# Two of the seven W2 operands of an attention + MLP kernel: read from stored bf16 copies, or cast from W2 by every pair

## The chip, the cores and the metric

The kernel runs on one core of a Trainium2 chip. The metric is the device time of one execution in microseconds (us), lower is better. Engines are named as the profile names them: PE (TensorE), PEld (its weight loads), DVE (VectorE), ACT (ScalarE), POOL (GpSimd), SP (SyncE, which here only issues DMAs).

## The reference

Eight batches of grouped-query attention (16 query heads, 4 key/value heads, 384 tokens, head size 64), whose output is the input of one MLP block:

```python
x   = softmax(q @ k^T / 8) @ v                     # per batch, then [384 tokens, 1024]
a1  = alpha1 * x + beta1
tok = einsum('ts,bsd->btd', w_tok, a1)
u   = x + lam * tok
a2  = alpha2 * u + beta2
ch  = relu(a2 @ w_ch1) @ w_ch2                     # w_ch1 [1024, 4096], w_ch2 [4096, 1024]
out = u + lam * ch
```

Inputs and output are float32. W1 and W2 below are `w_ch1` and `w_ch2`.

## The kernel before

**Pairs.** The batches are worked two at a time: four pairs (`ps`, and `i` in `pair`, 0 to 3). The two big matrix products of a pair are each done with seven half-size products in place of eight (Strassen's scheme with sums shared): the two batches are the halves on one side, and the four quarters of a weight matrix are those on the other. So each pair has a *first product* (activations by W1, relu) and a *second product* (by W2), each of seven parts numbered 1 to 7.

**First product of pairs 1 to 3** (`pair`, the loop over `g`, L818 to L864). Eight groups g = 0 to 7, each of 14 steps of four matmuls (`SEQ1`, L831). A group needs two W1 chunks of 512 KB (bf16 in SBUF), which POOL's DMAs read from the float32 W1 and cast on the way (`load_w1`, L183). They go into a ring `w1` of six slots; the loads for group g+3 are issued when group g gives its two slots back (`free`, `pump`). DVE makes the sums of W1 chunks for group g+1 while PE works on group g (`sum_w1`, L510 and L515, at steps k = 2, 5, 8 and 11). The two adds at L838 read the PSUM tiles `Y`, into which part 4, the last two steps of the group, accumulates further.

**Second product** (L876 to L941). Seven parts in the order of `PLACE2`: 1, 2, 6, 5, 3, 7, 4. Each needs an operand made of W2 (2 MB in bf16, four tiles of 512 KB): parts 1, 2 and 3 use the plain quarters "11", "21" and "22" of W2, the other four use differences of quarters. Pair 0 builds all of them: it loads the quarters with a cast (`load_w2`), DVE forms the differences (`sum_w2`), and SP writes every operand as bf16 into 28 tiles `w2s` in HBM (`keep_w2`, L494; quarter "21" goes there by a casting DMA, `cast_w2`). Pairs 1 to 3 read the tiles back in order n = 0 to 27 with SP's DMAs (`fetch`, L528), n // 4 being the place of the part in the order above: n = 0 to 3 are part 1, n = 16 to 19 part 3. They go into the six `w1` slots, which the first product gives back from group 5 on, and into three slots of `pad`.

**Where the order comes from.** The instruction order on every engine is the order of the program text (`tc.manual_schedule`). `queue` holds the W1 and W2 loads in one list; `pump` issues from its head whenever a slot is given back, at that point of the program. So a `fetch` stands in SP's stream (SP's queue) at the place where its slot was given back, and SP stops there until the slot is free; a `load_w1` stands likewise in POOL's. The rest comes from `plan`, a table of (pair, product, step): among others `load_next` (POOL's DMAs for k, q and v of the next two batches), and `put_flips`, which in the first product of pairs 0 to 2 puts on SP the transposing DMAs for the next batch's attention: `flip_k` (L170, all of kT, 12 blocks of 128 x 128) and four `flip_q` (L174, a quarter of qT each, 6 blocks). A `flip_q` can start when its quarter of `q_raw` has been loaded by POOL (L436). After the first product the attention of the next two batches is woven into the second product, batch 2 ps + 2 first. Pair 3 has no next pair, so it has no flips and no attention.

**DMA queues.** POOL's DMAs, casting ones and the accumulating stores to `out` (L442), are q0 (software_dynamic) in the profile; SP's plain loads, stores and transposes are q1 (hardware_dynamic). A DMA of SP or POOL also waits until the eighth DMA before it on the same engine has landed.

```python
queue += [(load_w1, c) for c in order1[4:]] + [(fetch, i, n) for n in range(SLOTS - 2)] + heads[:2]
...
put_flips(ps, 0, c, (44, 46, 50, 54, 58) if ps == 0 else range(76, 86, 2))
```

The five flips of pairs 1 and 2 thus stand at steps 76 to 84 of the first product's 112, in groups 5 and 6; group 5 gives its two slots back at steps 80 and 81.

Of the kernel before, what the change touches and what calls it, by code (L numbers as in the profile page):

```python
# [13 lines left out]
def kernel(  # L14
# [21 lines left out]
    nc = tc.nc  # L36
# [81 lines left out]
    SLOTS = 7 * NH // 4  # L118
    w2s = [tc.dram_tile([P, NDT * CW * P], bf, name=f"w2s{i}") for i in range(SLOTS)]
    PLACE2 = {o: i for i, o in enumerate((1, 2, 6, 5, 3, 7, 4))}  # L120

    def by_tok(ap):
        return ap.rearrange("(p st) d -> p st d", st=NST)
# [342 lines left out]
    raw = {}  # L466
# [4 lines left out]
    def w2_block(name, c):  # L471
        kh, dw = int(name[0]) - 1, int(name[1]) - 1
        return w2src[:, kh * NH + 4 * c:kh * NH + 4 * c + 4, dw * 512:(dw + 1) * 512]

    def stored(c):
        return w2s[4 * PLACE2[2] + c]

# [13 lines left out]
            nc.gpsimd.dma_start(out=at.rearrange("p (a c) -> p a c", a=4), in_=w2_block(name, c))  # L491

    def keep_w2(o, c):
        nc.sync.dma_start(out=w2s[4 * PLACE2[o] + c], in_=raw[{1: "11", 3: "22", 5: "12", 6: "12", 7: "11", 4: "again"}[o], c][1])  # L494

    def sum_w2(o, c):
        at = lambda name: raw[name, c][1]
        to, x, y = {5: ("12", "12", "11"), 6: ("12", "22", "12"), 7: ("11", "12", "11"), 4: ("again", "again", "12")}[o]
        tt(out=at(to), in0=at(x), in1=at(y), op=SUB)
        keep_w2(o, c)  # L500
# [17 lines left out]
    w2_slots, w2_at = {}, {}  # L518
# [3 lines left out]
    def place(slot):  # L522
        return ring[:, slot] if slot < RING else pad[:, (slot - RING) * 2048:(slot - RING + 1) * 2048]

    def fetch(i, n):
        w2_slots[i, n] = slot = (pad_free if n in PADDED else w1_free).pop(0)
        w2_at[i, n] = place(slot)
        nc.sync.dma_start(out=w2_at[i, n], in_=w2s[n])  # L528

    def free(slot):  # L530
        (w1_free if slot < RING else pad_free).append(slot)
# [46 lines left out]
    for i in range(1, NB):  # L578
        heads = [(load_w1, c) for c in order1[:4]] if i + 1 < NB else []
        queue += [(load_w1, c) for c in order1[4:]] + [(fetch, i, n) for n in range(SLOTS - 2)] + heads[:2]  # L580
        queue += [(fetch, i, n) for n in (SLOTS - 2, SLOTS - 1)] + heads[2:]
# [190 lines left out]
    def pair(i):  # L772
# [102 lines left out]
        where = {2: (0, 0), 3: (0, 1), 7: (1, 1), 4: (1, 0)}  # L875
        for k, o in enumerate(PLACE2):  # L876
            whole = not last and o != 4
# [69 lines left out]
    with tc.manual_schedule(engines=order):  # L947
# [123 lines left out]
        def put(ps, phase, at, *m):  # L1071
            plan.setdefault((ps, phase, at), []).append(m)
# [25 lines left out]
        for c in range(4):  # L1098
            put(0, 0, (50, 72, 74, 44)[c], load_w2, "11", c)
            put(0, 0, (6, 14, 42, 46)[c], cast_w2, "21", c)  # L1100
            put(0, 1, (41, 43, 45, 47)[c], keep_w2, 1, c)
            put(0, 1, 38 + 2 * c, keep_w2, 3, c)
            put(0, 1, (9, 10, 13, 15)[c], sum_w2, 5, c)
            put(0, 1, (20, 21, 25, 26)[c], sums_first_hid, 2, c)
            put(0, 1, (28, 30, 31, 34)[c], sums_first_hid, 4, c)
            put(0, 1, (37, 40, 41, 43)[c], sum_w2, 6, c)
            put(0, 1, (44, 45, 49, 50)[c], sums_first_hid, 3, c)
            put(0, 1, (51, 54, 57, 58)[c], sum_w2, 7, c)
            put(0, 1, (61, 64, 68, 71)[c], last_w2, c)
        for u, o in ((77, 5), (79, 7), (81, 6)):  # L1110
            put(0, 1, u, sum_w1, 0, o)
        for ps in range(NB - 1):
            c = 2 * ps + 2
# [100 lines left out]
```

## Time and profile before

| | |
|---|---|
| median of 3 runs | 732.88 us (731.51 to 733.32) |
| the profiled execution's own time | 731.92 us |
| its span, first to last instruction | 729.9 us |
| PE busy | 717.4 us |
| DVE, ACT, POOL busy | 543.9, 373.8, 199.2 us |
| q0: packets, MB, share of 16 engines | 109872, 64.47, 65.4% |
| q1: packets, MB, share of 16 engines | 86988, 87.42, 42.8% |
| granted TensorE clock | 1.000 |

Times inside the span are us from its start. First products of pairs 1, 2 and 3 begin at about 234, 408 and 581, their second products at about 307, 480 and 654. A share of DMA time can be over 100%, because the packets of one engine overlap. "To landing" is from a DMA's issue to its arrival.

### The profile page before, as it was taken

What the parts mean: (1) busy time and instruction counts of PE and PEld (TensorE: products, weight loads), DVE (VectorE), ACT (ScalarE), POOL (GpSimd) and SP (SyncE); (2) the same over time, 40 slices, a digit from 0 to 9 for tenths busy, and PEclk for the clock granted to TensorE, in tenths of its full rate; (3) what the DMA queues carried; (4) which work ended last, traced back from release to release, by engine and by line L of the source; (5) the groups of instructions that cost most, each with busy time, mean ns of one, the idle gap of its engine ahead of it and who ended that gap; (6) DMA issues with size and microseconds to landing.
All of it is one profiled execution on the core that took longest, in us unless ns stands there. A gap on an engine that the chain in (4) does not pass through costs nothing.

```text
span 729.9 us, 14511 instructions
## 1 busy us (share of the span) xinstructions
PE 717.4 (98%) x5716; PEld 408.7 (56%) x5716; DVE 543.9 (75%) x1009; ACT 373.8 (51%) x566; POOL 199.2 (27%) x242
## 2 busy tenths in 40 slices
PE   8899999999999999999999999999999999999998
PEld 4665555555555666555555566655555566654444
DVE  7888876577888988649678888748868988763354
ACT  7877666544563666643433466663333366650000
POOL 8844233221046551201022344200002222000011
PEclk9999999999999999999999999999999999999999
DMA  9999999999999999969989999998989999937965
GB/s 164 180 239 231 190 195 227 226 242 235 366 312 232 179 182 196 234 221 207 272 193 220 160 162 194 212 227 201 270 233 183 210 126 146 165 123 264 302 174 104
DMA packets 197616, 153.26 MB, mean 210 GB/s; under 512 B 90540, under 2 KB 175892, under 8 KB 197292
## 3 DMA queue, kind: packets, MB, share of 16 engines
q0 software_dynamic: 109872, 64.47, 65.4%
q1 hardware_dynamic: 86988, 87.42, 42.8%
q8 instruction: 44, 0.72, 0.4%
q10 hardware_dynamic: 688, 0.46, 0.2%
q14 instruction: 24, 0.20, 0.1%
HBM read 155.23 MB, written 39.85 MB: 267 GB/s over the span
## 4 chain that ended last, share of the span: by engine, by line
PE 90%; DVE 4%; POOL 2%; DMA 1%; issue 1%; ACT 1%; DVEq 0%; ACTq 0%; POOLq 0%
PE C L897 30%; PE X L831 17%; PE C L752 10%; PE Y L831 9%; PE Z L831 4%; PE sc L260 4%; PE X L681 4%; PE sc L295 3%; PE sc L324 3%; PE Y L681 3%; DMA ops<-obuf 1%; DVE pad L565 1%; PE Z L681 1%; PE tok L324 1%; POOL obuf L334 0%
## 5 line engine op out<-in xcount | busy, mean ns | idle before, releaser
L897 PE MATMUL C<-w,arena 128*128 128x512 bf16 (+2 forms) x744 | 168.3, 372 | 0.0
L269 ACT ACTIVATE es<-sc 128x1024 bf16<-128x1024 f32 x108 | 104.1, 1024 | 116.0 <-PE sc L260 107.6
L897 PEld LDWEIGHTS <-arena 128*128 128x128 bf16 x1040 | 94.8, 98 | 100.5 <-issue 5.1
L442 POOL DMA_DIRECT2D out_dram<-hT x45 | 40.0, 888 | 294.7 <-DVE hT L790 135.9
L836 ACT ACTIVATE hT<-X,bias 128x384 f32<-128x384 f32 x144 | 83.6, 582 | 60.0 <-PE X L831 55.2
L831 PEld LDWEIGHTS <-w 128*128 128x128 bf16 x768 | 75.1, 98 | 50.0
L831 PEld LDWEIGHTS <-pad 128*128 128x128 bf16 x576 | 56.4, 98 | 37.2
L183 POOL DMA_DIRECT2D w<-in_moe_w_ch_dram x48 | 45.4, 1002 | 105.6 <-PE X L831 36.5
L831 PE MATMUL X<-ops,w 128*128 128x384 bf16 x384 | 70.3, 326 | 0.0
L831 PE MATMUL X<-ops,pad 128*128 128x384 bf16 x384 | 70.3, 326 | 0.0
L897 PE MATMUL C<-pad,arena 128*128 128x512 bf16 (+2 forms) x296 | 70.2, 373 | 0.0
L324 PEld LDWEIGHTS <-wtokT 128*128 128x128 bf16 x576 | 39.0, 98 | 16.4 <-issue 3.4
L752 PEld LDWEIGHTS <-arena 128*128 128x128 bf16 x336 | 29.8, 98 | 30.0 <-issue 2.5
L331 DVE TENSOR_TENSOR xr<-sc,xr 128x384 f32<-128x384 f32 x48 | 26.5, 553 | 25.6 <-PE sc L324 14.3
L752 PE MATMUL C<-w,arena 128*128 128x512 bf16 x168 | 41.2, 379 | 0.0
L838 DVE TENSOR_TENSOR arena<-Y,hT 128x384 bf16<-128x384 f32 x48 | 26.5, 556 | 17.7 <-ACT hT L836 16.0
L295 PEld LDWEIGHTS <-es 128*128 128x128 bf16 x864 | 32.8, 97 | 11.3
L831 PE MATMUL Y<-ops,w 128*128 128x384 bf16 x192 | 39.1, 326 | 0.0
L831 PE MATMUL Z<-ops,w 128*128 128x384 bf16 x192 | 39.0, 326 | 0.0
L269 ACT ACTIVATE hT<-sc 128x1024 bf16<-128x1024 f32 x36 | 35.8, 1031 | 4.3 <-PE sc L260 4.0
L260 PE MATMUL sc<-qT,kT 64*128 64x384 bf16 (+2 forms) x504 | 37.2, 271 | 0.5 <-ACT hT L269 0.2
L842 ACT ACTIVATE arena<-X,bias 128x384 bf16<-128x384 f32 x48 | 27.9, 582 | 17.7 <-PE X L831 16.1
(190 smaller groups left out, 1175.1 us busy)
## 6 DMA issues: line engine op xcount, KB each, us to landing
w<-w2s SPq DMA_DIRECT2D x67, 512.0 KB, 5.1
w<-in_moe_w_ch_dram POOLq DMA_DIRECT2D x65, 512.0 KB, 9.8
pad<-w2s SPq DMA_DIRECT2D x25, 512.0 KB, 6.9
out_dram<-hT POOLq DMA_DIRECT2D x45, 256.0 KB, 7.1
out_dram<-xr SPq DMA_DIRECT2D x48, 192.0 KB, 5.3
q_raw<-in_q_dram POOLq DMA_DIRECT2D x28, 192.0 KB, 9.5
w2s<-w SPq DMA_DIRECT2D x10, 512.0 KB, 7.6
arena<-in_moe_w_ch_dram POOLq DMA_DIRECT2D x8, 512.0 KB, 15.9
```

Source lines behind the costliest of these rows:

```text
L183: nc.gpsimd.dma_start(out=w1[:, w1_slots[c]], in_=w1src[:, :, c * CW * P:(c + 1) * CW * P])
L260: nc.tensor.matmul(out=sc[:, hh, k % 4:k % 4 + n], lhsT=kT_[r, 2 * p // G, BLK[hh][sk], :], rhs=qT_[r, p, st:st + n, :], start=True, stop= ...
L269: nc.scalar.activation(out=e, in_=sc, func=EXP, scale=scale_qk)
L295: nc.tensor.matmul(out=av[:, hh, sq, :], lhsT=ess[k // 4][:, m % 2, k % 4, :], rhs=vb[:, sk, hk, :], start=(sk == 0), stop=(sk == NST - 1))
L324: nc.tensor.matmul(out=ps[:, tt, :], lhsT=wtokT[:, st, tt * P:(tt + 1) * P], rhs=a1s[p][:, st, :], start=(st == 0), stop=(st == NST - 1 an ...
L442: nc.gpsimd.dma_start(out=by_tok(out[b])[:, ms, dw * 512:(dw + 1) * 512], in_=o, accum_op=ADD)
L681: nc.tensor.matmul(out=ps[:, :n], lhsT=tb[G, o][:, dt, e * P:(e + 1) * P], rhs=opb(FIRST1[o], n)[:, dt], start=(o in (1, 2, 7) and dt == 0 ...
L752: nc.tensor.matmul(out=x, lhsT=lead_hid[:, t, FIRST2[o], ms * P:(ms + 1) * P], rhs=rhs[:, t % 4 * 512:(t % 4 + 1) * 512], start=(o in (1, ...
L831: nc.tensor.matmul(out=ps, lhsT=tb[g, o][:, dt, e * P:(e + 1) * P], rhs=opb(LEFT1[o])[:, dt], start=(o in (1, 2, 7) and dt == 0), stop=(dt ...
L836: nc.scalar.activation(out=snap[o, e], in_=ps, func=IDENT, bias=hi if o == 5 else lo)
L842: nc.scalar.activation(out=hid[:, t, 4], in_=ps, func=RELU, bias=hi)
L897: nc.tensor.matmul(out=x, lhsT=hid[:, t, LEFT2[o], ms * P:(ms + 1) * P], rhs=rhs[:, t % 4 * 512 + c0:t % 4 * 512 + c1], start=((not last o ...
```

## The change

The eight `keep_w2` calls for products 1 and 3 in pair 0 are gone. In pairs 1 to 3 `fetch` reads the eight tiles of those products not from `w2s` but from the float32 W2, with a casting DMA, which POOL issues. These are 24 loads of 512 KB (as they arrive; 1 MB as they are read) that leave SP's stream and join POOL's; the instructions of PE, DVE and ACT stay in their order.

```diff
     PLACE2 = {o: i for i, o in enumerate((1, 2, 6, 5, 3, 7, 4))}
+    RAW2 = {PLACE2[1]: "11", PLACE2[3]: "22"}
...
     def keep_w2(o, c):
-        nc.sync.dma_start(out=w2s[4 * PLACE2[o] + c], in_=raw[{1: "11", 3: "22", 5: "12", 6: "12", 7: "11", 4: "again"}[o], c][1])
+        nc.sync.dma_start(out=w2s[4 * PLACE2[o] + c], in_=raw[{5: "12", 6: "12", 7: "11", 4: "again"}[o], c][1])
...
         w2_at[i, n] = place(slot)
-        nc.sync.dma_start(out=w2_at[i, n], in_=w2s[n])
+        if n // 4 in RAW2:
+            nc.gpsimd.dma_start(out=w2_at[i, n].rearrange("p (a c) -> p a c", a=4), in_=w2_block(RAW2[n // 4], n % 4))
+        else:
+            nc.sync.dma_start(out=w2_at[i, n], in_=w2s[n])
...
             put(0, 0, (6, 14, 42, 46)[c], cast_w2, "21", c)
-            put(0, 1, (41, 43, 45, 47)[c], keep_w2, 1, c)
-            put(0, 1, 38 + 2 * c, keep_w2, 3, c)
```

`w2_block(name, c)` is the view of the float32 W2 that pair 0's own loads use.

## The prediction

> **What bounds the kernel now.** I read the busy times of the page first:
>
> ```profile
> span 729.9 us, 14511 instructions
> PE 717.4 (98%) x5716; PEld 408.7 (56%) x5716; DVE 543.9 (75%) x1009; ACT 373.8 (51%) x566; POOL 199.2 (27%) x242
> ```
>
> PE is the bound, and going through its timeline for gaps I find none between 225 and 726 us. So the change cannot gain anything in pairs 1 to 3; it can only open a gap there. The stalls it could remove lie in pair 0's second product: 0.59 us before the matmul at 204.89 (behind ACT L269), 0.24 us at 221.20 (ACT L269 again), 0.95 us at 224.76 (behind DVE L309). Together 1.8 us.
>
> Next, who stands behind the moved loads: SP's timeline in the first product of pair 1.
>
> ```profile
> 253.25 4.27 SPq L170 DMA_TRANSPOSE kT<-k  x1
> 257.61 2.81 SPq L174 DMA_TRANSPOSE qT<-q_raw  x1
> 287.23 0.34 SPq L528 DMA_DIRECT2D w<-w2s  x1
> 287.66 1.22 SPq L174 DMA_TRANSPOSE qT<-q_raw  x1
> 289.04 0.45 SPq L528 DMA_DIRECT2D w<-w2s  x1
> 289.59 3.13 SPq L174 DMA_TRANSPOSE qT<-q_raw  x2
> ```
>
> SP stops at 260.4 for W2 tile n = 0, whose slot PE frees at 287.2, and three `flip_q` stand behind it. Their data come much sooner: the second and third q_raw load, issued at 252.9 and 253.6, take 14.2 us to landing (median of the two), the fourth, issued at 262.0, 13.9 us; so they are there at about 266, 269 and 276. In pair 2 it is the same: SP stops from 429.7 to 460.4 with three flips behind it, whose data arrive at about 440, 441 and 448.
>
> What a flip costs the POOL queue shows in the DMA view by stretches of 12 us; first 256 to 268, with `flip_k` and one `flip_q`, then 438 to 450, with no flip:
>
> ```profile
> q0 software_dynamic: 2978, 1.54, 96.8%
> q1 hardware_dynamic: 2271, 0.57, 41.1%
> ```
>
> ```profile
> q0 software_dynamic: 4697, 2.34, 145.2%
> ```
>
> With 18 blocks of transposes beside it, q0 moves 1.54 MB in place of 2.34 MB. And q0 carries the W1 loads of the first product. The second load of a group's two, issued at 416.07, 425.62 and 270.46:
>
> ```profile
> w<-in_moe_w_ch_dram POOLq DMA_DIRECT2D x1, 512.0 KB, 7.7
> ```
>
> ```profile
> w<-in_moe_w_ch_dram POOLq DMA_DIRECT2D x1, 512.0 KB, 12.9
> ```
>
> ```profile
> w<-in_moe_w_ch_dram POOLq DMA_DIRECT2D x1, 512.0 KB, 12.4
> ```
>
> 7.7 us ahead of pair 2's `flip_k`, 12.9 us beside it; from there on q0 is never empty until the first product's last W1 load (12.5, 12.2 and 9.8 us for the next three). How near to the limit that is, DVE's timeline in group 4 of pair 1 shows:
>
> ```profile
> 274.86 0.69 DVE L515 TENSOR_TENSOR pad<-w 128x1024 bf16<-128x1024 bf16 x1 [0.61 <-DMA w<-in_moe_w_ch_dram]
> 275.58 0.69 DVE L510 TENSOR_TENSOR w<-w 128x1024 bf16<-128x1024 bf16 x1
> 276.20 0.56 DVE L838 TENSOR_TENSOR arena<-Y,hT 128x384 bf16<-128x384 f32 x1
> 276.68 0.68 DVE L1040 TENSOR_TENSOR vecs<-vecs 128x512 f32<-128x512 f32 x1
> 277.28 0.55 DVE L838 TENSOR_TENSOR arena<-Y,hT 128x384 bf16<-128x384 f32 x1
> ```
>
> The sum for group 5 waited 0.61 us for W1 already, and behind it stand the two reads of `Y` (L838), which part 4 on PE must wait for. PE's timeline has that part of group 5:
>
> ```profile
> 287.68 1.46 PE L831 MATMUL Y<-ops,pad 128*128 128x384 bf16 x8
> ```
>
> Groups repeat every 9.10 us, so in group 4 part 4 starts at 278.58 and its second half, which needs the second L838, at 279.23. That L838 ended at 277.83: 1.40 us are left.
>
> **The change, part by part.** *Eight `keep_w2` fewer in pair 0.* SP issues eight 512 KB stores less between 179 and 198. DVE waits 1.10 us at 204.10 for such a store, but its next operations wait for PE and ACT anyway. The stalls at 204.89 and 221.20 are ACT's queue of exponentials, and that at 224.76 is DVE held while POOL multiplies at L790; POOL's run of these follows a W1 load that waits for DVE's sum at 210.17, not for a store. I take 0, with bounds 0 and -1.8.
>
> *24 loads on POOL's queue.* Price of one: three W2 casts of pair 0 issued at 127.97, 128.71 and 129.64 land after 11.4, 13.2 and 15.1 us, that is 2.6 and 2.8 us apart; the issue takes 0.75 us of POOL. Part 3 (n = 16 to 19): slots come free in pair 2 at 509 to 524, the part starts at 538.35, so each load has at least 17 us, and even 15.1 us is in time. In pair 3, 17 us and more. Part 1 (n = 0 to 3): its tightest are n = 2 and 3, freed at 296.3 and 297.0 and needed at 309.8 and 310.6, 13.5 us. A W1 load into an empty q0 took 5.9 us (407.18). Behind them wait the k, q and v loads of the batch after next; q, the first needed, is used at 321.7 and landed by 306. I take 0 for all 24.
>
> *Three `flip_q` released early, in pairs 1 and 2.* The flips now follow SP's first `flip_q` directly and start when their data land: 266, 269 and 276 plus delay in pair 1, 440 to 441 and 448 plus delay in pair 2. They are 18 blocks, as many as `flip_k` and one `flip_q`, so they take from q0 what these took. From the two stretches: 0.80 MB at 2.34 MB per 12 us is 4.1 us; the stretch 426 to 438, also with 18 blocks, shows q0 at 1.27 MB, 5.5 us. I take the middle, 4.8 us, two thirds of it (3.2) by the W1 loads of group 5, all by those of group 6.
>
> Pair 1, group 4: W1 for group 5 landed at 274.8 (issued at 261.1, 13.7 to landing), now 3.2 later; less the 1.40 left, PE stalls 1.8 us. Group 5: W1 for group 6 landed at 282.9 (270.46 + 12.4), now 287.7. DVE wanted it at 283.26 and now, 1.8 later, at 285.1: a wait of 2.6. From that sum to the end of the second L838 are 2.97 us (as above, 274.86 to 277.83), so without a wait it ends at 286.23 and PE needs it at 287.68 + 0.65 = 288.33; 2.1 us are covered, 0.5 stalls. Group 6: W1 for group 7 lands at 289.1 + 4.8 = 293.9, wanted at 292.4 + 2.3: no wait. Pair 1: 2.3 us.
>
> Pair 2, group 4: W1 landed at 447.3, now 450.5, wanted at 447.36: 3.1 of wait, of which 2.5 are covered (no L1040 in this pair; first L838 then ends 1.90 after the sum's start, and part 4 starts at 451.78), 0.6 stalls. Group 5: 456.1 + 4.8 = 460.9, wanted at 456.46 + 0.6: 3.8, less 2.5, 1.3. Pair 2: 1.9 us. Pair 3 has no flips.
>
> Sum: +4.2 us. With 4.1 us of q0 per pair the same steps give 1.6 + 1.2 = 2.8; with 5.5, 3.0 + 2.6 = 5.6. Against the profiled execution's own 731.92 that is 736.1; the median of the runs is 0.96 above it, so I predict 737.1.
>
> **A rule against the change.** The Trainium skill, page "SBUF — State Buffer", section "SBUF: two separate sides", says that a DMA issued from GpSimd is held while VectorE holds the port they share, since its descriptors cannot be written, and gives about 3.1 us in place of 0.62 us for one. The row that bears on it: between 269 and 281 us DVE is busy almost without a break, and W1's DMAs still issue in 0.88 to 0.93 us each. By the rule, an estimate from that page, each W2 load could come 2.5 us later than I take it, and four in a row would be late for part 1, the case of rival 2.
>
> **The rivals.** (1) *The flips collide, but PE does not feel it:* 732.9. For: in group 0 of pair 1 DVE waited 2.92 us for W1 at 238.07 and PE had no gap; three flips might also fit between W1's packets. Against: 1.40 us of cover in group 4. It decides if q0 loses under 2 us per pair. Chance 0.25. (2) *W2 arrives late:* if n = 2 and 3 take the 15.1 us of pair 0's slowest cast, n = 3 is 1.5 us late for part 1 in each of pairs 1 and 2; with the flips' 4.2 that gives 740.1. Against: by my sum W1 for group 7 lands at 293.9, then come four W2 loads at 2.7 us and two k loads at 1.0 us (landing at 290.1 and 291.1 before), so n = 3 lands near 306.7 and is needed at 310.6 + 2.3 = 312.9. Chance 0.08, counted with the flips. (3) *Faster:* SP's backlog in pair 0 sets the three PE stalls. For: SP issues there about every 1.2 us from 183 to 206 without waiting for anything that the profile names, and DVE did wait for one store. Against: what PE next needs from DVE there, L331 at 205.85, waited for PE's own matmuls (L324 and L328 up to 205.72). If so, and if the flips hide, PE gains 1.8 us: 731.1. It decides only where q0 loses under 2 us per pair, and is over 0.3% only if the stretch hides more than its gaps show: chance 0.05. (4) *The flips stay late:* if a wait other than n = 0's slot held them, nothing would change in pairs 1 and 2. In the changed order no load stands ahead of them, and `flip_k`'s and the first flip's waits were over at 260: counted in rival 1.
>
> **How the numbers follow.** The flips' collision over PE's cover (alone or with late W2) has 0.70, no visible effect 0.25, a gain 0.05. 0.3% is 2.2 us, about what a measurement of this kernel can tell from no change; my lower bound of 2.8 us clears it. The range goes from 732.0, which takes in rival 1 with half of pair 0's 1.8 us, to rival 2's 740.1; the likeliest case alone spans 735.7 to 738.5. Faster 0.05, same 0.27, slower 0.68, a little of the 0.70 falling short of 2.2 us.
>
> **What would show it.** On SP, `flip_q` two to four at about 266, 269 and 279, ahead of any L528; in pair 2 at 440, 441 and 451. The W1 loads of groups 5 and 6 landing 3 to 5 us later after issue. DVE's L515 waiting for W1 2 to 4 us, twice in each of the two pairs. PE gaps at `Y<-ops,pad`, released by DVE L838, 4.2 us in all, and none at the start of parts 1 and 3. I am wrong if the flips stay behind 287, if q0 loses under 2 us, or if PE's new gaps stand at L897.

## The result and the profile after

| | before | after |
|---|---|---|
| median | 732.56 us (731.16 to 736.41, 13 runs) | 738.28 us (735.39 to 747.42, 13 runs) |
| profiled execution | 731.92 us, span 729.9 | 736.10 us, span 733.9 |

The ratio is 1.0079, 95% interval 1.0059 to 1.0099: slower, by 5.7 us in the medians and 4.2 us between the profiled executions. The forecast was 737.1 us, slower. Some profiled executions below ran at a granted clock under 1.000 (the first of `early_flips` at 0.859, its second and `held_again` at 0.995); of these no whole span is compared, only what happens inside a product.

In the changed kernel the lines behind the insertions have moved: L831, L838, L844 and L897 are now L835, L842, L848 and L901; L515 is L516; the flips are L171 and L175; SP's `fetch` is L532 and POOL's casting one L530.

The page's busy times and queues of the changed kernel (packets, MB, share of 16 engines):

```profile
span 733.9 us, 14505 instructions
PE 718.9 (98%) x5716; PEld 408.9 (56%) x5716; DVE 541.8 (74%) x1009; ACT 373.9 (51%) x566; POOL 217.4 (30%) x266
...
q0 software_dynamic: 122544, 77.05, 76.0%
q1 hardware_dynamic: 82380, 70.64, 36.3%
```

q0 has 12.6 MB more and q1 16.8 MB less, and POOL its 24 instructions more (18.2 us). PE does the same matmuls, so the 4 us more of span are time between them. SP's timeline in pair 1's first product shows what stands where it used to wait for n = 0:

```profile
252.49 3.62 SPq L171 DMA_TRANSPOSE kT<-k  x1
256.21 23.24 SPq L175 DMA_TRANSPOSE qT<-q_raw  x4
307.42 0.97 SPq L532 DMA_DIRECT2D w<-w2s  x2
```

The four `flip_q` are one uninterrupted row. Taken apart, they start at 256.21, 265.66, 267.82 and 278.24, and SP's first W2 fetch (now n = 4) comes at 307.42. In pair 2 the last three start at 441.22, 442.52 and 452.54. The DMA view of the changed kernel, at the second W1 loads for groups 5, 6 and 7 of pair 1 (issued at 260.44, 269.79 and 278.78; last column: us to landing):

```profile
w<-in_moe_w_ch_dram POOLq DMA_DIRECT2D x1, 512.0 KB, 16.6
```

```profile
w<-in_moe_w_ch_dram POOLq DMA_DIRECT2D x1, 512.0 KB, 16.8
```

```profile
w<-in_moe_w_ch_dram POOLq DMA_DIRECT2D x1, 512.0 KB, 14.0
```

They took 13.7, 12.4 and 9.8 us before. Who waits for that is in DVE's timeline, group 4 of pair 1:

```profile
277.11 0.69 DVE L516 TENSOR_TENSOR pad<-w 128x1024 bf16<-128x1024 bf16 x1 [3.53 <-DMA w<-in_moe_w_ch_dram]
277.84 0.69 DVE L511 TENSOR_TENSOR w<-w 128x1024 bf16<-128x1024 bf16 x1
278.45 0.55 DVE L842 TENSOR_TENSOR arena<-Y,hT 128x384 bf16<-128x384 f32 x1
278.91 0.68 DVE L1044 TENSOR_TENSOR vecs<-vecs 128x512 f32<-128x512 f32 x1
279.51 0.55 DVE L842 TENSOR_TENSOR arena<-Y,hT 128x384 bf16<-128x384 f32 x1
```

and in PE's:

```profile
277.26 0.81 PE L835 MATMUL Z<-ops,w 128*128 128x384 bf16 x4
279.05 0.81 PE L835 MATMUL Y<-ops,pad 128*128 128x384 bf16 x4 [0.97 <-DVE arena L842]
280.12 0.81 PE L835 MATMUL Y<-ops,pad 128*128 128x384 bf16 x4 [0.26 <-DVE arena L842]
280.76 1.46 PE L835 MATMUL X<-ops,w 128*128 128x384 bf16 x8
282.72 0.81 PE L835 MATMUL Y<-ops,w 128*128 128x384 bf16 x4 [0.49 <-DVE arena L848]
```

The wait for W1 is 3.53 us where it was 0.61, so the two reads of `Y` at L842 come 2.9 us later in the product, and PE, with 1.40 us of cover, starts part 4 1.55 us late, in two halves. Once more PE waits, at 282.72: behind L848, DVE's read of `Y` after part 4, which the next group needs before it may write that buffer. The ends of matmuls are modelled, so a gap in brackets shows less than is lost. The sums below go by starts: how much later a matmul starts, counted from the first matmul of its product, than the same matmul of the kernel before.

By starts, the first products of this execution lost 2.66 us in pair 1 and 0.76 in pair 2. Pair 3's first product and the second products of pairs 1 and 2 lost nothing. Pair 3's second product lost 1.27 us, at one place, W2 tile n = 19 of part 3:

```profile
702.95 1.03 PE L901 MATMUL C<-w,arena 128*128 128x512 bf16 x4
705.09 2.10 PE L901 MATMUL C<-w,arena 128*128 128x512 bf16 x9 [1.11 <-DMA w<-in_moe_w_ch_dram]
```

Pair 0 ended 0.66 us earlier. The sum, 4.03, is the difference of the spans (4.0).

### The profile page after: what moved, and what is told of

It reads as the page before. It is cut to its first block, busy times and chain, and to the rows that moved or that the text cites. A ratio compares the mean times of both kernels' runs of the same rounds, so it can differ in the third digit from the quotient of the medians.

```text
span 733.9 us, 14505 instructions
## 1 busy us (share of the span) xinstructions
PE 718.9 (98%) x5716; PEld 408.9 (56%) x5716; DVE 541.8 (74%) x1009; ACT 373.9 (51%) x566; POOL 217.4 (30%) x266
## 4 chain that ended last, share of the span: by engine, by line
PE 70%; DMA 10%; issue 7%; POOL 6%; DVE 5%; ACT 1%; POOLq 0%; ACTq 0%; DVEq 0%
PE C L901 26%; PE X L835 9%; DMA w<-in_moe_w_ch_dram 9%; PE C L756 8%; PE Y L835 4%; PE sc L261 4%; PE X L685 4%; PE sc L296 3%; PE sc L325 3%; PE Y L685 3%; PE Z L835 2%; DMA q_raw<-in_q_dram 2%; POOL hT L794 1%; PE E L617 1%; POOL w L184 1%
## 5 line engine op out<-in xcount | busy, mean ns | idle before, releaser
L901 PE MATMUL C<-w,arena 128*128 128x512 bf16 (+2 forms) x744 | 168.5, 372 | 1.1 <-DMA w<-in_moe_w_ch_dram 1.1
L901 PEld LDWEIGHTS <-arena 128*128 128x128 bf16 x1040 | 94.7, 98 | 101.8 <-issue 6.5
L835 PEld LDWEIGHTS <-w 128*128 128x128 bf16 x768 | 75.1, 98 | 51.6 <-issue 1.8
L835 PEld LDWEIGHTS <-pad 128*128 128x128 bf16 x576 | 56.3, 98 | 39.1 <-issue 2.0
L835 PE MATMUL X<-ops,w 128*128 128x384 bf16 x384 | 70.2, 326 | 0.0
L835 PE MATMUL X<-ops,pad 128*128 128x384 bf16 x384 | 70.2, 326 | 0.0
L901 PE MATMUL C<-pad,arena 128*128 128x512 bf16 (+2 forms) x296 | 70.2, 373 | 0.0
L756 PE MATMUL C<-w,arena 128*128 128x512 bf16 x168 | 41.2, 379 | 0.0
L835 PE MATMUL Y<-ops,w 128*128 128x384 bf16 x192 | 39.0, 326 | 1.1 <-DVE arena L848 1.1
L835 PE MATMUL Z<-ops,w 128*128 128x384 bf16 x192 | 39.0, 326 | 0.0
L842 DVE TENSOR_TENSOR arena<-Y,hT 128x384 bf16<-128x384 f32 x48 | 26.4, 556 | 16.1 <-ACT hT L840 14.5
## 6 DMA issues: line engine op xcount, KB each, us to landing
arena<-in_moe_w_ch_dram POOLq DMA_DIRECT2D x8, 512.0 KB, 16.8
```

The source lines that it names most:

```text
L756: nc.tensor.matmul(out=x, lhsT=lead_hid[:, t, FIRST2[o], ms * P:(ms + 1) * P], rhs=rhs[:, t % 4 * 512:(t % 4 + 1) * 512], start=(o in (1, ...
L835: nc.tensor.matmul(out=ps, lhsT=tb[g, o][:, dt, e * P:(e + 1) * P], rhs=opb(LEFT1[o])[:, dt], start=(o in (1, 2, 7) and dt == 0), stop=(dt ...
L901: nc.tensor.matmul(out=x, lhsT=hid[:, t, LEFT2[o], ms * P:(ms + 1) * P], rhs=rhs[:, t % 4 * 512 + c0:t % 4 * 512 + c1], start=((not last o ...
```

## The experiments

Theory: the three released flips take q0's time from W1, and DVE and then PE come late; the casting loads cost nothing. Main rival: the 24 casting loads on POOL's queue cost the time, about equally. The first four kernels ran together, beside 35 runs of the kernel before (median 732.57); the next four beside 23 runs (median 734.29), the last three, each profiled once, beside one (735.42). A ratio is the one on record, and not the quotient of two medians: for part 1 alone, below, the medians give 1.0075 where the record has 1.0053.

**The flips alone.** W2 stays as before; only the places of the flips in pairs 1 and 2 change:

```diff
-            put_flips(ps, 0, c, (44, 46, 50, 54, 58) if ps == 0 else range(76, 86, 2))
+            put_flips(ps, 0, c, (44, 46, 50, 54, 58) if ps == 0 else range(70, 80, 2))
```

> The kernel before, W2 read from the stored bf16 tiles by SP as ever; only the five flips of pairs 1 and 2 stand ten to six steps earlier in the program, so that no W2 load is ahead of them on SP. Theory (the released flips take q0's time from W1): flip_q two to four at about 266, 269 and 278 us, PE gaps at Y<-ops,pad in groups 4 and 5, pair 1's first product 2.0 to 2.7 us longer, pair 2's 0.8 to 1.9, in all 2.8 to 4.6 us over before. Rival (the casting loads are what costs): no casting load is added, so within 0.5 us of before and no new gap.

Measured: 739.55 us median (lowest 736.17, 12 runs), ratio 1.0084 (1.0047 to 1.0122). Pairs 1 to 3 cast no W2 here, and the slowdown is as large as that of the whole change, 1.0079. By the medians it is 7.0 us, more than the 2.8 to 4.6 expected. A second execution was profiled for its trace:

> The kernel before with the three flip_q of pairs 1 and 2 put ahead of W2 tile n = 0's fetch on SP, profiled a second time for its trace. By the theory of the flips: flips at about 266, 268 and 278 and at 441, 442 and 452, W1 for groups 5 and 6 landing 14 to 17 us after issue, first products of pairs 1 and 2 longer by 2 to 4 us each, PE's gaps at Y behind DVE's reads of Y, none behind a DMA. Rival (something else that the changed kernel does costs the time): first products of 72.8 us.

In it pair 1's first product begins at 242.47, so I count from there: the three flips start at 33.0, 35.1 and 45.4 us, in the changed kernel at 31.9, 34.1 and 44.5. Its PE timeline has the same two halves of part 4:

```profile
288.63 0.81 PE L831 MATMUL Y<-ops,pad 128*128 128x384 bf16 x4 [1.80 <-DVE arena L838]
289.69 0.81 PE L831 MATMUL Y<-ops,pad 128*128 128x384 bf16 x4 [0.25 <-DVE arena L838]
```

Pair 1's first product lost 3.37 us, within the expected 2 to 4; pair 2's lost 0.40, below it.

**The change without the release.** A small DMA into the first 64 bytes of each partition of n = 0's slot, which the cast then overwrites, makes SP wait for that part of the slot:

```diff
         w2_at[i, n] = place(slot)
+        if n == 0 and i < NB - 1:
+            nc.sync.dma_start(out=w2_at[i, n][:, :32], in_=w2s[4][:, :32])
         if n // 4 in RAW2:
```

> The kernel after, all 24 casting loads kept; in pairs 1 and 2 SP writes 64 bytes per partition of a stored tile into tile n = 0's slot first, and so waits for that slot as before the change, with flip_q two to four behind it. Theory: the flips go back behind 287 and 460, the gaps in the first products vanish, and what is left is the late part 3 of pair 3 (1.1 us before the matmul at 705 in the trace of after): 1.0 to 2.0 us over before. Rival (the casting loads cost in themselves, through HBM or POOL): as slow as after, 5 to 6 us over before.

Measured: 732.10 us (731.56 to 736.59, 12 runs), ratio 0.9977 (0.9947 to 1.0006). All 24 casting loads are in, and nothing is lost. SP's timeline (L530 is the small DMA here):

```profile
256.57 2.72 SPq L175 DMA_TRANSPOSE qT<-q_raw  x1
281.06 0.34 SPq L530 DMA_DIRECT2D w<-w2s  x1
281.50 6.40 SPq L175 DMA_TRANSPOSE qT<-q_raw  x3
```

and DVE's, where the sum for group 5 waits 0.23 us:

```profile
274.11 0.69 DVE L516 TENSOR_TENSOR pad<-w 128x1024 bf16<-128x1024 bf16 x1 [0.23 <-DMA w<-in_moe_w_ch_dram]
```

SP's wait ended at 281.06, 6 us sooner than the 287 expected: by the code, the last to read the columns that the small DMA writes is the first matmul of part 7 in group 5, and it starts at 280.70. It was late enough. The flips run from 281.5 to 288, beside W1 for group 7, whose sum starts 57.98 us into the first product, as before: the same transposes cost nothing where the load beside them has slack. The loss that I expected in pair 3 did not come: n = 19 landed 13.7 us after issue, in time.

**One part cast, the other stored.**

```diff
-    RAW2 = {PLACE2[1]: "11", PLACE2[3]: "22"}
+    RAW2 = {PLACE2[1]: "11"}                      # part1_only; keep_w2 of product 3 is back
+    RAW2 = {PLACE2[3]: "22"}                      # part3_only; keep_w2 of product 1 is back
```

> Only part 1's operand is cast by every pair; part 3's is stored and read back as before. Theory: the flips are released (n = 0 is no longer on SP), pair 3's part 3 is in time: 2.8 to 4.6 us over before, gaps at Y<-ops,pad in pairs 1 and 2, none at L901 (L897 of before). Rival (each casting load costs the same): half of after's excess, 2.9 us, wherever it stands; then part3_only has the same.

> Only part 3's operand is cast by every pair; part 1's is stored and read back as before. Theory: n = 0 is still on SP, so the flips stay behind 287 and 460 and the first products have no gap; pair 3's tile n = 19 is late by about 1.1 us: 1.0 to 2.0 us over before. Rival (each casting load costs the same): 2.9 us over before.

Measured: part 1 alone 738.06 us (736.23 to 739.89), ratio 1.0053 (1.0024 to 1.0081); part 3 alone 732.38 us, ratio 0.9980 (0.9949 to 1.0011). The two have 12 casting loads each. Only part 1's takes n = 0 out of SP's stream, and it has the whole loss: 3.54 and 3.73 us in the two first products of the profiled execution, and 5.5 us by the medians, both more than the 2.8 to 4.6 expected. The rival is refuted: by it part 3 alone would have lost as much. The loss expected of part 3 did not come.

**One or two flips released.** In the kernel before, the places of the five flips become

```diff
+ (76, 78, 79, 82, 84)     # one_flip: one flip_q more ahead of n = 0
+ (76, 78, 79, 79, 84)     # two_flips: two more
```

> The kernel before, with only the second flip_q of pairs 1 and 2 put ahead of W2 tile n = 0's fetch on SP; the third and fourth stay behind it. Theory of a cover (the flips take 0.27 us of q0 per block, and PE feels only what exceeds the 1.40 us left in pair 1 and the 2.5 us in pair 2): 6 blocks take 1.6 us; pair 1 loses 0.2 us, pair 2 nothing, together +0.2 us, within 0.3% of before; W1 for group 5 lands 1 to 2 us later in both pairs. Rival, a cost in proportion to the blocks (a third of the 5.7 us by which the medians of the changed kernel and of before differ): +1.9 us.

> The kernel before, with the second and third flip_q of pairs 1 and 2 put ahead of W2 tile n = 0's fetch on SP; the fourth stays behind it. Theory of a cover: 12 blocks take 3.2 us of q0, all ahead of W1 for group 5; pair 1 loses 3.2 - 1.4 = 1.8 us, pair 2 3.1 - 2.5 = 0.6 us, group 6's loads are covered: +2.4 us. Rival, in proportion to the blocks: two thirds of 5.7, +3.8 us. If the fourth flip, beside the W1 loads for group 6, is what costs, +0 to 0.5 us.

Measured: one 735.30 us, ratio 1.0011 (0.9984 to 1.0039); two 735.52 us, ratio 1.0020 (0.9992 to 1.0048). On 734.29 us these intervals are -1.2 to +2.9 and -0.6 to +3.5 us. The first holds both expectations, the second the cover's +2.4 and not +3.8, though only just; by the times alone this stays open. The traces are plainer: one flip cost 0.08 us in pair 1's group 4 and 0.65 in group 5, two cost 1.78 and 0.64, and neither cost pair 2 anything. So one flip cost 0.73 us where the cover had 0.2; the section on the prediction says why. W1 for group 5 came 1.4 us later after issue in pair 1 and 0.8 in pair 2 with one flip, 3.1 and 1.8 with two: in pair 1 about what 6 and 12 blocks were to take (1.6 and 3.2), in pair 2 about half of it.

**The changed kernel twice more, and once more the two kernels that had lost nothing.** These ask whether pair 3's late tile is regular, and how steady the rest is.

> The changed kernel itself, profiled a second time. If the W2 tile n = 19 of pair 3 is late for part 3 by the casting loads' own price, it lands 17 to 18 us after issue again and PE waits about 1 us near 705; if that was a chance of one execution, it lands after 13 to 15 us, as it does with the casting part 3 alone, and PE waits 0. First products of pairs 1 and 2 longer than 72.8 us by 2 to 4 and 0.5 to 4 us.

> The changed kernel profiled a third time. PE's loss in group 4 of pairs 1 and 2 is what W1's second load for group 5 lands later than 41.8 us after the first product's start, in each pair by itself, 0 if it lands earlier; n = 19 in pair 3 lands 18 us after issue and PE waits 1.1 to 1.4 us at part 3, if that is regular.

> The changed kernel with the flips held back once more, profiled a second time. From pair 3's start its instructions are those of the changed kernel. If W2 tile n = 19 is late in pair 3 by the casts' own price, it lands 18 us after issue, as in the two profiles of the changed kernel; if it belongs to executions in which the first products of pairs 1 and 2 ran late, it lands after 13.7 us again. First products of 73.0 us from first matmul to last.

> Only part 3 cast by pairs 1 to 3, profiled a second time. n = 19 in pair 3: 18 us after issue if late by its own price, 13.8 us if not. First products of 73.0 us from first matmul to last.

The changed kernel took 738.07 and 736.61 us (spans 736.1 and 733.8), `held_again` 737.72 and `part3_again` 731.44. The expectation of `after_third` held: in pairs 1 and 2 W1 for group 5 landed 43.93 and 41.81 us into the first product, 2.1 and 0.0 us past the 41.8, and group 4 lost 2.17 and 0. By starts, the three executions of the changed kernel lost, against the kernel before:

| execution | pair 0 | first product, pair 1 | first product, pair 2 | second product, pair 3 | sum |
|---|---|---|---|---|---|
| the first | -0.66 | 2.66 | 0.76 | 1.27 | 4.03 |
| `after_again` | -0.54 | 2.01 | 3.23 | 1.53 | 6.23 |
| `after_third` | -0.49 | 3.18 | 1.21 | 0.01 | 3.91 |

W2 tile n = 19 of pair 3 landed 18.0, 18.3 and 15.2 us after issue in these three; PE waited for it in two. The DMA view of `after_again` and then of `after_third` at that load:

```profile
w<-in_moe_w_ch_dram POOLq DMA_DIRECT2D x1, 512.0 KB, 18.3
```

```profile
w<-in_moe_w_ch_dram POOLq DMA_DIRECT2D x1, 512.0 KB, 15.2
```

In the two executions of each of `held_flips` and `part3_only` it took 13.5 to 13.8 us, although their instructions in pair 3's second product are the same. So it is neither the price of the loads themselves nor regular; what makes it is open.

`held_again` lost nothing in pairs 1 to 3. `part3_again`, whose three flips wait behind n = 0 as before the change, lost 0.42 us in pair 2's first product, in group 5, against the expectation of none:

```profile
449.14 0.69 DVE L516 TENSOR_TENSOR pad<-w 128x1024 bf16<-128x1024 bf16 x1 [2.36 <-DMA w<-in_moe_w_ch_dram]
```

There the k that `flip_k` waits for had landed 19.6 us into the first product, where the kernel before has 17.2, and the first `flip_q` started at 25.7 in place of 19.7. So W1 can come late for pair 2 without any released flip; why k came late is open.

## Why the prediction was right, and where it was off

*What bounds the kernel.* Right: all that was lost in pairs 1 to 3 is a gap of PE.

*Pair 0, taken at 0.* The three PE stalls stand in the changed kernel's trace at 204.22, 220.53 and 224.09 with their old lengths of 0.59, 0.24 and 0.95 us, so the eight stores did not set them. That pair 0 ended 0.5 to 0.7 us sooner is no effect of the change that the runs can tell: `two_flips`, which leaves pair 0 alone, began its pair 1 at 233.67, the kernel before at 234.38, the changed one at 233.72.

*24 loads on POOL, taken at 0.* Right for part 1. In pair 1 its tiles n = 2 and 3 landed 5.4 and 7.2 us after issue, at 303.9 and 306.5 (I had n = 3 near 306.7), and PE had no gap there. The k, q and v loads behind them had landed by 314.4, q by 310.7. Off for part 3 in pair 3: 17 us were to be enough, and two executions of three took 18. The term I put at 0 measured 1.3, 1.5 and 0.0 us.

That was also the place that would have proved me wrong (new gaps at L897, now L901). It did not carry the result: the flips alone give the whole ratio. The rule of the Trainium skill that I weighed ("SBUF — State Buffer", section "SBUF: two separate sides") is not seen at work: the casts for part 1 in pair 1 and for part 3 in pair 3 each held POOL 0.74 to 0.78 us, as the 0.75 in pair 0. The longest of the 24 in that trace held it 1.11 us.

*The flips' release.* Right in place, and in pair 1 in size. Forecast starts 266, 269, 279 and 440, 441, 451; measured 265.7, 267.8, 278.2 and 441.2, 442.5, 452.5. W1 in pair 1 was to come 3.2 and 4.8 us later after issue and came 2.9 and 4.4 later; in pair 2 1.6 and 3.1 in place of 3.2 and 4.8. Over the three executions it was 2.4 to 3.5 and 3.7 to 4.9 in pair 1, 1.6 to 4.2 and 3.1 to 4.4 in pair 2.

*The cover.* This is the step on which the forecast stood, and it can be tested with every trace. The prediction says that PE loses in group 4 what DVE's sum for group 5 starts later than 1.40 us past 274.86 in pair 1, that is 41.88 us after the first product's start; in pair 2 2.5 us past 447.36, that is 42.28 us. Where the sum started, and what group 4 lost by PE's starts:

| execution, pair | sum starts | by the rule | lost |
|---|---|---|---|
| before, 1 and 2 | 40.47, 39.78 | 0, 0 | 0, 0 |
| after, 1 and 2 | 43.39, 41.71 | 1.51, 0 | 1.55, 0 |
| `after_again`, 1 and 2 | 42.97, 44.33 | 1.09, 2.05 | 1.12, 2.07 |
| `after_third`, 1 and 2 | 44.02, 42.26 | 2.14, 0 | 2.17, 0 |
| `part1_only`, 1 and 2 | 44.39, 44.44 | 2.51, 2.16 | 2.55, 2.18 |
| `early_flips_b`, 1 and 2 | 44.22, 41.26 | 2.34, 0 | 2.37, 0 |
| `two_flips`, 1 and 2 | 43.62, 41.58 | 1.74, 0 | 1.78, 0 |
| `held_flips`, 1 and 2 | 40.21, 39.95 | 0, 0 | 0, 0 |
| `held_again`, 1 and 2 | 39.90, 40.42 | 0, 0 | 0, 0 |
| `part3_only`, 1 and 2 | 39.90, 40.71 | 0, 0 | 0, 0 |
| `part3_again`, 1 and 2 | 39.90, 42.22 | 0, 0 | 0, 0 |

(`one_flip` fits too, less the 0.96 us that its pair 1 lost in group 0, ahead of every flip: 42.88 - 0.96 is 0.04 over the limit, and it lost 0.08.) The rule holds within 0.04 us in each row. The proportional cost does not: with the same three flips pair 2's group 4 lost nothing in three executions and 2 us in two.

Those 2 us are not all the released flips'. In `after_again` 0.72 and in `part1_only` 0.40 us of them stand at group 4's first `Y`, behind a late sum for group 4. Its W1 had landed at 32.7 and 32.4 us, before the second `flip_q` started at 34.6 and 34.1. In these two the k that `flip_k` waits for had landed at 18.5 and 17.9, and `flip_k` and the first `flip_q` started late; in the other executions, `part3_again` and the first of `early_flips` apart, it landed at 17.0 to 17.4. That the late k makes the difference is not tested.

*Mis-sized: what follows group 4.* I had 0.5 and 1.3 us in group 5, at part 4, and nothing in group 6. In the three executions of the changed kernel group 5 lost 0.64 or 0.65 in pair 1 and 0.29 to 0.74 in pair 2, group 6 0.24 to 0.46. In pair 1 none of this stands at part 4: as the PE lines show for the first execution, it is the next group's first `Y` behind L848; DVE's wait for W1 in group 5 was 1.20 us there, not 2.6, and covered. In pair 2 0.24 to 0.30 us of it stand at part 4, the rest at a first `Y` too. I followed DVE's lateness only to the reads at L838; the reads at L844, a few operations on, are as late, and the group after needs them. That is the step that was missing, and the kernel before shows its size. DVE's first read at L844 in group 4 of pair 1, and the first `Y` of group 5 on PE:

```profile
279.88 0.55 DVE L844 TENSOR_TENSOR arena<-Y,hT 128x384 bf16<-128x384 f32 x1
```

```profile
281.18 0.81 PE L831 MATMUL Y<-ops,w 128*128 128x384 bf16 x4
```

The read ends at 280.43, so 0.75 us are left and not 1.40, and the sum for group 5 must start by 41.22 us and not by 41.88. With this limit groups 4 and 5 of pair 1 together should lose 2.17, 1.75 and 2.80 us in the three executions of the changed kernel; they lost 2.20, 1.77 and 2.81. For `part1_only`, `early_flips_b` and `two_flips` it gives 3.17, 3.00 and 2.40, measured 3.20, 3.02 and 2.42; for `one_flip` 0.70, measured 0.73. In pair 2 the first `Y` of group 5 came late in four executions (`after_again`, `after_third`, `part1_only`, `part3_again`), and each puts the limit at 41.8 us, 2.0 us of cover in place of 2.5. Group 6's loss is absent in `one_flip` and `two_flips`, so it belongs to the fourth flip, which these two leave behind n = 0.

*The sum.* 4.2 us forecast in pairs 1 and 2 (2.3 and 1.9); the three executions lost 3.4, 5.2 and 4.4 (means 2.6 and 1.7). That this came so near is partly luck. In pair 2 one execution lost 3.23 us and another 0.76. And of the three sums only 1.9, 2.7 and 2.5 us stand at `Y<-ops,pad`, where the forecast had all of it; the rest stands at the reader that it left out. The median of 738.28 lies 1.2 us above the forecast; pair 3's late tile, 0.9 us in the mean of three, is about that much.

*The rivals.* No visible effect (1) fell with `early_flips`. Late W2 (2) did not occur at part 1, where I put it, though at part 3 a smaller form did. Faster (3) and flips that stay late (4) fell: the three PE stalls stayed, and the flips moved.

`held_flips` keeps the change and takes its cost away. That it would beat the kernel before is not shown: its interval reaches 1.0006, and the kernel before had no gap in these stretches to close.

## What to carry to other kernels

A DMA that waits in an in-order queue is also a schedule for what stands behind it; when it is moved to another queue, ask first what that wait held back, and what the released transfers will run beside. Price the released work as lateness of the transfer it collides with, and follow the waiting engine's lateness past the first consumer, to every later operation that another engine needs: the cover to subtract is the smallest of theirs (here, in pair 1, 0.75 us and not 1.40). If the collision costs, hold the released work at a place where the transfer beside it has slack, rather than undo the change.

## What the runs showed of the hardware that was not expected

The same program with the same three flips delivered W1 for pair 2's group 5 at 41.2, 43.9 and 41.8 us into the first product in three executions, each at a granted clock of 1.000. With 2.0 us of cover there, groups 4 and 5 of that pair lost 0.29, 2.76 and 0.74 us, so one profile can't size such a collision. A 512 KB casting load of W2 took 5.4 to 9.2 us to landing at part 1 of pair 1 in the six traces that have it, and 13.5 to 18.3 us as n = 19 of pair 3, behind three other casts and beside SP's loads.
